# Fused attention and two MoE layers on one core: a second PSUM bank for the rows of w3·w_out, k of a head pair by one transfer, a scheduler that knows banks, and early operands for block 3

## Chip, cores and metric

One core of one Trainium2 chip. The metric is the device time of one launch in microseconds; three runs of the kernel before are given. TensorE's two clock levels are 1.2 and 2.4 GHz; the profile shows the granted share (1.00 is 2.4 GHz).

## The reference, cut

```python
attn_out = _attn_ref(q, k, v)            # (4, 8, 576, 64), block-causal, blocks of 64
x = attn_out.transpose(0, 2, 1, 3).reshape(2304, 512)
a, b = x @ w1, x @ w2                    # 512 -> 1024
h = a * b @ w3                           # 1024 -> 1024
y = h @ w_out                            # 1024 -> 512
r = np.maximum(y @ moe2_w_in, 0.0)       # 512 -> 2048
out = (r * r) @ moe2_w_out               # 2048 -> 512
```

The weights arrive as float64 and are taken apart on the chip into float32, and from there into a high and a low part.

## The kernel before

**Setup.** w3 and w_out are multiplied once: `setup_rows(i)` makes row block i (0 to 7) of w3·w_out, 128 x 512, by products of `w3_t[i]` with the eight pieces of w_out, accumulated in one PSUM bank. Rows 0 to 2 multiply in fp32 (8 products), rows 3 to 7 in three products of high and low parts each (24). Rows 0 to 5 (`PO_SPLIT = 6`) share the single buffer of tag `po`; of these rows 1 to 5 are made in two halves of 256 columns of that bank, each with its own eviction: ACT copies the high part into `w3o` (L1209), DVE the low part (L1214). Rows 6 and 7 take a bank from `bank3`, which goes round three banks: two of tag `tp`, one of tag `po`.

**Attention.** A head pair p (0 to 15) is loaded by `load_pair` (q, k, v; k as two transfers of 64 partitions, L627), its scores are made in groups of query tiles (`pair`), and pairs 0 to 3, those of batch b = 0, transpose their fp32 weights on TensorE: `transpose` makes for each pair, group and head a main and a last part, 48 tiles of tag `tp` with two buffers, each copied out by ACT (L974). Later pairs transpose by DMA. `attend` multiplies with v, into the bank `pv_bank`.

**First MoE.** `first_block(b)` makes a·b from the `w12` tiles (`ab`) and multiplies with the eight rows (`y`); y goes to DRAM. `w12_tile` converts w1 and w2; each has a small product on TensorE with column sums (`norm_scale`, L357, into `pv_bank`).

**Second MoE.** `second_block` goes over y in five blocks (`BLOCKS`: one of 256 tokens, c = 0, then four of 512). For c = 1 to 4 `h_winograd` makes seven products per pair j of weight tiles (`p17`, `p26`, `p45` with two halves each, `p3`) from operands that `y_load` splits out of y: `b11`, `b21`, `b22` and the differences `t1` to `t4`, each as a high part (ACT, L275) and a low part (DVE, L277). Each operand has one buffer. For c from 2 on the second product is `out_strassen` (`p1` to `p7` with a block number only). The products of `h_winograd` go round the three banks of `bank3`.

**What sets the order.** Nothing is issued as written. `Order.op` collects operations with an engine, an estimated cost, keys for what they read and write, and a priority; `Order.emit` then runs a list scheduler over all of them: on each engine it takes, among the operations whose inputs are ready at the earliest start, the one with the lowest priority key, and issues it. Each engine (and the queues of SP and POOL) then works in that order. `PE` work of low priority (rows, `ab`, `y`) fills where attention is not ready. `warm_up` puts idle matmuls of a zero tile where the scheduler sees TensorE idle in the first microseconds, into a buffer of tag `po`. An operation waits for a bank only through its keys: the two halves of a row have keys of their own, `(bank, half)`.

```python
        if not i:
            po_bank.append(buf("pm", "po", 1, [P, 512], F32, "po"))
        for half in range(2) if 0 < i < PO_SPLIT else (None,):
```

Of the kernel before, what the change touches and what calls it, by code (L numbers as in the profile page):

```python
# [7 lines left out]
F32 = mybir.dt.float32  # L8
F32R = mybir.dt.float32r
BF16 = mybir.dt.bfloat16  # L10
F16 = mybir.dt.float16
# [35 lines left out]

class Buf:
# [18 lines left out]
class Op:  # L67
    def __init__(self, eng, cost, fn, key, spare):
        self.eng, self.cost, self.fn, self.key, self.spare = eng, cost, fn, key, spare
        self.deps = set()  # L70
        self.left = 0
        self.users = []
        self.ready = 0.0
        self.end = None


class Order:
# [19 lines left out]
    def op(self, eng, cost, fn, r=(), w=(), key=0.0, spare=0.0):  # L97

        o = Op(eng, cost, fn, key, spare)
        o.same = self.same.get(eng, 0.0)  # L100
        for k in r:
            if k in self.writer:
                o.deps.add(self.writer[k])
            self.readers.setdefault(k, []).append(o)
        for k in w:
            if k in self.writer:
                o.deps.add(self.writer[k])
            o.deps.update(self.readers.pop(k, ()))
            self.writer[k] = o
        for k in list(r) + list(w):  # L110
            if isinstance(k[0], Buf):
                k[0].ops.append(o)
        o.deps.discard(o)
        self.ops.append(o)
        return o

    def emit(self):
# [11 lines left out]
        free, avail, dma = {}, {}, 0.0  # L129
        for n, o in enumerate(self.ops):  # L130
            o.n = n
            if not o.left:
                avail.setdefault(o.eng, []).append(o)
        count = 0
        while True:
            best = None
            for eng, todo in avail.items():
# [3 lines left out]
                start = max(t0, min(o.ready for o in todo))  # L141
                o = min((o for o in todo if o.ready <= start), key=lambda o: (o.key, o.n))
# [14 lines left out]
            else:  # L157
                free[eng] = start + o.cost
                o.end = free[eng] + self.TAIL.get(eng, 0.0)
            o.fn()  # L160
# [10 lines left out]
def fused_kernel(ctx: ExitStack, tc: tile.TileContext, qT, kT, vp, va, w12, w3t, wo, wb, out):  # L171
# [388 lines left out]

    raws = {}
# [20 lines left out]
    warm_out = buf("pm", "po", 1, [P, 512], F32, "warm_out")  # L582
# [33 lines left out]
    def load_pair(p):  # L616
# [7 lines left out]
        for a in range(2):  # L624
            rows = slice(64 * a, 64 * a + 64)
            od.op(
                GQ, c_dma(144), lambda rows=rows, n=2 * p + a: pool.dma_start(out=k()[rows], in_=kT[n][0:64]),  # L627
                [], [(k, a)], key,
            )
# [321 lines left out]
    def transpose(p, g, a, pf, weights, key):  # L951
# [7 lines left out]
        for part, (todo, n) in enumerate(((mains, P), (lasts, 64))):  # L959
            tp = buf("pm", "tp", 2, [P, 512], F32, f"tp_{name}_{part}")  # L960
# [154 lines left out]
    def bank3(name):  # L1115

        n_bank3[0] += 1
        tag, n = ("po", 1) if n_bank3[0] % 3 == 0 else ("tp", 2)
        return buf("pm", tag, n, [P, 512], F32, name)
# [53 lines left out]
    def setup_rows(i):  # L1173
# [4 lines left out]
        if not i:  # L1178
            po_bank.append(buf("pm", "po", 1, [P, 512], F32, "po"))
        for half in range(2) if 0 < i < PO_SPLIT else (None,):  # L1180
            cols = slice(0, 512) if half is None else slice(256 * half, 256 * half + 256)
            n = cols.stop - cols.start
            if i < PO_SPLIT:
                acc = Half(po_bank[0], cols, range(2) if half is None else (half,))
# [184 lines left out]
    def second_block():  # L1369
# [33 lines left out]
        ys_ = {}  # L1403
        raws_ = {}
        r_ = {}
        cp_ = {}

        def y_part(c, name):

            home = "wp" if name in ("b11", "b21") else "w2"  # L1410
            return [late(f"{name}{n}", [P, 2, TH], f"{name}{n}_{c}", F16, 1, home) for n in "hl"]

        def y_split(c, name, src, key):
            h, l = ys_[c, name] = y_part(c, name)
            split_half(h, l, src, 2 * TH, ([(h,)], [(l,)], [key]), K_EVICT)
# [106 lines left out]
        def y_load(c):  # L1522
# [17 lines left out]
            def sub(o, x, y, r, w):  # L1540
                od.op(
                    DVE, c_dve(2 * TH),
                    lambda: dve.tensor_tensor(out=o(), in0=x(), in1=y(), op=ALU.subtract), r, w, K_EVICT,
# [216 lines left out]
        def h_direct(c, j, key):  # L1760
            gt = g_half(c, j, f"g2_{c}_{j}")
            bt = beta_a if j < SOON else beta
            for k in range(2):
# [11 lines left out]
                ks = both(f, 0) + [(t,) for x in ("b11", "b21") for t in ys_[c, x]]  # L1775
# [66 lines left out]
        def h_winograd(c, j, key):  # L1842
# [16 lines left out]
            def product(acc, half, left, yname, spare=0.3):  # L1859
# [11 lines left out]
                od.op(PE, len(mms) * c_mm16(TH), go, ks + [(t,) for t in y], [(acc, half)], key, spare * strassen)  # L1871
# [30 lines left out]
            product(b17, 1, s_of(3), "t3")  # L1902
# [4 lines left out]
            product(b26, 1, s_of(2), "t2")  # L1907
            if strassen:
# [433 lines left out]
```

## Time and profile before

| | |
|---|---|
| three runs | 858.09, 859.74 and 859.10 us, median 859.1 us |
| the profiled execution | 859.63 us, of which the span from first to last instruction is 857.9 us |
| busy in the span | PE 834.0 us, PEld 676.9 us, DVE 704.3 us, ACT 605.3 us, POOL 111.4 us |
| granted TensorE clock, mean | 0.998 |

The profile is of one execution. Engines: PE TensorE's matmuls, PEld its weight loads (beside PE), DVE VectorE, ACT ScalarE, POOL GpSimd, SP the queue of SyncE. L12 is line 12 of the kernel before. An fp32 product is recorded as two matmuls. A time in brackets is idle time of the engine just before the row, with what ended it. PE's ends are modelled, so gaps under a few tenths of a microsecond do not show as idle.

### The profile page before, as it was taken

The numbers are of one execution on the slowest core, as the hardware profiler recorded it, in microseconds if no ns is written. First come the engines' busy times: TensorE is split into PE (matmuls) and PEld (weight loads), VectorE is DVE, ScalarE is ACT, GpSimd is POOL, SyncE is SP. The second block draws the span as 40 slices with busy tenths as digits, with TensorE's granted clock in tenths as the row PEclk, the third lists the DMA queues.
The fourth block names the chain that finished last, engine by engine and source line by source line (L and its number), as shares of the span: only waits on it lengthen the run. The fifth ranks groups of instructions, "written<-read, shape, count | busy, mean of one in ns | idle before, by whom it ended". The sixth has DMA issues, their size and how long they took to land. (4 is left out here: it accounts for less than half of the span.)

```text
span 857.9 us, 19317 instructions
## 1 busy us (share of the span) xinstructions
PE 834.0 (97%) x7504; PEld 676.9 (79%) x7504; DVE 704.3 (82%) x1643; ACT 605.3 (71%) x1393; POOL 111.4 (13%) x206
## 2 busy tenths in 40 slices
PE   8999999999999999999999999999999999999997
PEld 6567776778878888789979878666678888888886
DVE  5988989997787787864788899999979798797775
ACT  5988888976677676764999985756755654664562
POOL 5111211111211112001322101010020001001000
PEclk9999999999999999999999999999999999999999
DMA  8942465699998999772665512020030002001001
GB/s 312 339 150 93 135 176 161 143 182 191 215 178 159 196 154 202 134 148 77 210 193 191 176 50 74 26 100 2 1 109 16 1 2 74 2 1 51 1 2 50
DMA packets 104830, 100.23 MB, mean 117 GB/s; under 512 B 83041, under 2 KB 86881, under 8 KB 103329
## 3 DMA queue, kind: packets, MB, share of 16 engines
q0 software_dynamic: 18144, 71.18, 26.5%
q1 hardware_dynamic: 86592, 27.80, 19.1%
q8 instruction: 59, 0.97, 0.5%
q14 instruction: 35, 0.28, 0.1%
HBM read 62.78 MB, written 9.44 MB: 84 GB/s over the span
## 5 line engine op out<-in xcount | busy, mean ns | idle before, releaser
L1108 PEld LDWEIGHTS <-w 128*128 128x128 f16 x1536 | 146.8, 98 | 43.7 <-issue 5.9
L884 ACT ACTIVATE pf<-s,nm 128x192 f32<-128x192 f32 (+4 forms) x160 | 82.4, 524 | 44.0 <-DVE nm L867 39.5
L1108 PE MATMUL ab<-x0h,w 128*128 128x320 f16 x512 | 108.9, 299 | 0.5 <-DVE w L287 0.3
L1108 PE MATMUL y<-g,w3o 128*128 128x320 f32 (+1 forms) x768 | 108.3, 298 | 0.0
L1108 PEld LDWEIGHTS y<-g,w3o 128*128 128x128 f32 x768 | 103.1, 188 | 2.1 <-issue 1.2
L1108 PE MATMUL ab<-x1h,w 128*128 128x256 f16 x512 | 88.7, 273 | 0.0
L2034 PEld LDWEIGHTS <-gs 128*128 128x128 f16 x816 | 78.9, 98 | 11.4 <-DVE gs L277 2.2
L1866 PEld LDWEIGHTS <-wb 128*128 128x128 f16 x768 | 75.1, 98 | 15.2 <-issue 3.8
L1108 PE MATMUL ab<-x0l,w 128*128 128x320 f16 x256 | 76.5, 299 | 0.7 <-DVE x0l L1033 0.7
L1929 ACT ACTIVATE c<-c,beta 128x512 f32<-128x512 f32 x48 | 34.2, 713 | 58.4 <-DVE c L1898 58.4
L932 DVE SCALAR_TENSOR_TENSOR p<-pf,r,p 128x192 f16<-128x192 f32 (+2 forms) x120 | 63.0, 546 | 12.5 <-ACT p L925 11.2
L1108 PE MATMUL ab<-x1l,w 128*128 128x256 f16 x256 | 69.8, 272 | 0.0
L2161 PE MATMUL o<-wb,g 128*128 128x512 f16 x288 | 66.7, 379 | 0.6 <-DVE c L2171 0.6
L925 ACT ACTIVATE p<-pf,r 128x192 f16<-128x192 f32 (+2 forms) x120 | 62.0, 556 | 6.6 <-DMA pt<-p 3.7
L2034 PE MATMUL p<-ts,gs 128*128 128x256 f16 x480 | 61.8, 273 | 0.1
L1866 PEld LDWEIGHTS <-st 128*128 128x128 f16 x576 | 56.1, 98 | 6.7
L825 PE MATMUL s<-kraw,qraw 64*128 64x288 f32 (+4 forms) x384 | 56.5, 411 | 0.4 <-ACT pf L884 0.2
L2161 PEld LDWEIGHTS <-g 128*128 128x128 f16 x288 | 27.9, 98 | 30.3 <-issue 0.9
L825 PEld LDWEIGHTS s<-kraw,qraw 64*128 64x128 f32 x384 | 34.2, 186 | 17.1 <-issue 8.3
L2034 PE MATMUL p<-wb,gs 128*128 128x256 f16 x336 | 44.7, 273 | 0.2 <-DVE gs L277 0.2
L859 DVE TENSOR_REDUCE nm<-s 128x2 f32<-128x384 f32 (+1 forms) x64 | 42.3, 683 | 1.0
L338 DVE CUSTOM_DVE_ANT_0 cx<-raw,cx 128x1024 uint16<-128x1024 uint16 (+1 forms) x53 | 39.0, 737 | 4.5 <-ACT raw L329 2.3
(265 smaller groups left out, 1977.4 us busy)
## 6 DMA issues: line engine op xcount, KB each, us to landing
raw<-in_wb POOLq DMA_DIRECT2D x32, 512.0 KB, 5.5
raw<-in_w3t POOLq DMA_DIRECT2D x8, 1024.0 KB, 10.0
raw<-in_w POOLq DMA_DIRECT2D x16, 512.0 KB, 4.8
yraw<-ydram POOLq DMA_DIRECT2D x12, 512.0 KB, 4.5
vraw<-in_vp POOLq DMA_DIRECT2D x16, 320.0 KB, 5.3
qraw<-in_qT POOLq DMA_DIRECT2D x16, 288.0 KB, 4.7
kraw<-in_kT POOLq DMA_DIRECT2D x32, 144.0 KB, 5.9
vmix<-v SPq DMA_DIRECT2D x24, 160.0 KB, 5.0
```

The costliest lines, as they stand in the source:

```text
L338: dve.tensor_tensor(out=x(), in0=x(), in1=words()[1], op=ALU.add)
L825: pe.matmul(o[:, h] if t == 4 else o, q()[rows, q_start(t) : q_start(t) + 128], keys_()[rows, c], start=True, stop=True,)
L859: lambda k=k, t=t, nm=nm, banks=banks: dve.tensor_reduce(out=nm()[:, k], in_=banks[0]()[:, :, S_COL[t] : S_COL[t] + n_keys(t)], op=ALU.max ...
L884: act.activation(o, view(a, t), AF.Exp, bias=nm()[:, k, a : a + 1], scale=SCALE, accum_out=ssum()[:, k, a : a + 1],)
L925: lambda o=o, nk=nk, a=a, k=k, w=weights, p16=p16, r=r: act.activation(p16()[:, o : o + nk], w(a, k), AF.Copy, scale=r()[:, k, a : a + 1]),
L932: lambda o=o, nk=nk, a=a, k=k, w=weights, p16=p16, r=r: dve.scalar_tensor_tensor(out=p16()[:, o + nk : o + 2 * nk], in0=w(a, k), scalar=r( ...
L1108: pe.matmul(acc(), l, r, start=k == 0, stop=k == len(mms) - 1)
L1866: pe.matmul(acc()[:, TH * half : TH * half + TH], lhs(a, kc), y[yn]()[:, kc], start=n == 0, stop=n == len(mms) - 1,)
L1929: lambda src=src, k=k: act.activation(src(), src(), AF.Relu, scale=beta()[:, j, k : k + 1]),
L2034: pe.matmul(acc()[:, TH * u : TH * u + TH], t()[:, o : o + P], r(b), start=first and n == 0 and u == tiles[0], stop=last and n == 2 and u ...
L2161: pe.matmul(o(), g[gx]()[:, cols], wt(f)[:, a, 512:1024], start=(begin and n == 0), stop=(last and n == 2),)
```

## The change

1. Tag `po` has two buffers and tag `tp` one (`bank3` keeps its round over the three). Each of rows 0 to 5 takes a `po` buffer of its own and is made whole, 512 columns wide, with one eviction on ACT and one on DVE.
2. k of a pair is loaded by one transfer of 128 partitions; the bytes are the same.
3. `Order` notes which PSUM buffers an operation touches and starts none while another engine's operation on the same buffer runs.
4. Operands of blocks 3 and 4 are split at a priority inside the block before (`K_LOAD`) instead of the highest; block 3's `b11`, `b21` and `t3` get buffers of their own (`OTHER_HOMES`), so they need not wait for block 2's.
5. In `h_winograd` the product `t3` (second half of `p17`) is put behind both halves of `p26`.

```diff
+        o.banks = tuple(dict.fromkeys(k[0] for k in (*r, *w) if isinstance(k[0], Buf) and k[0].pool in PSUM_POOLS))
...
+        held = {}
+
+        def at(o):
+            t = o.ready
+            for b in o.banks:
+                for e, until in held.get(b, {}).items():
+                    if e != o.eng and until > t:
+                        t = until
+            return t
...
-                start = max(t0, min(o.ready for o in todo))
-                o = min((o for o in todo if o.ready <= start), key=lambda o: (o.key, o.n))
+                start = max(t0, min(at(o) for o in todo))
+                o = min((o for o in todo if at(o) <= start), key=lambda o: (o.key, o.n))
...
+            for b in o.banks:
+                held.setdefault(b, {})[eng] = o.end + self.WAIT
...
-    warm_out = buf("pm", "po", 1, [P, 512], F32, "warm_out")
+    warm_out = buf("pm", "po", 2, [P, 512], F32, "warm_out")
...
-        for a in range(2):
-            rows = slice(64 * a, 64 * a + 64)
-            od.op(
-                GQ, c_dma(144), lambda rows=rows, n=2 * p + a: pool.dma_start(out=k()[rows], in_=kT[n][0:64]),
-                [], [(k, a)], key,
-            )
+        both = slice(2 * p * P + P // 2, 2 * p * P + P // 2 + P)
+        od.op(GQ, c_dma(288), lambda: pool.dma_start(out=k(), in_=k_rows[both]), [], [(k, 0), (k, 1)], key)
...
-            tp = buf("pm", "tp", 2, [P, 512], F32, f"tp_{name}_{part}")
+            tp = buf("pm", "tp", 1, [P, 512], F32, f"tp_{name}_{part}")
...
-        tag, n = ("po", 1) if n_bank3[0] % 3 == 0 else ("tp", 2)
+        tag, n = ("tp", 1) if n_bank3[0] % 3 == 0 else ("po", 2)
...
-        if not i:
-            po_bank.append(buf("pm", "po", 1, [P, 512], F32, "po"))
-        for half in range(2) if 0 < i < PO_SPLIT else (None,):
+        if i < PO_SPLIT:
+            po_bank.append(buf("pm", "po", 2, [P, 512], F32, f"po_{i}"))
+        for half in (None,):
...
-                acc = Half(po_bank[0], cols, range(2) if half is None else (half,))
+                acc = Half(po_bank[i], cols, range(2) if half is None else (half,))
...
+        K_LOAD = [K_EVICT if c < 3 else K_B + 2 * (KP * (c - 1) + 5) + 0.55 for c in range(len(BLOCKS))]
...
+        OTHER_HOMES = {
+            "b11": ("wp", "ysq", 1, 1), "b21": ("wp", "ysc", 1, 1), "t3": ("mo1", "a", 2, 2),
+        }
...
-            split_half(h, l, src, 2 * TH, ([(h,)], [(l,)], [key]), K_EVICT)
+            split_half(h, l, src, 2 * TH, ([key_of(h)], [key_of(l)], [key]), K_LOAD[c])
...
             product(b17, 0, w_of(0, 0), "b11")
-            product(b17, 1, s_of(3), "t3")
...
             product(b26, 0, w_of(0, 1), "b21")
             product(b26, 1, s_of(2), "t2")
+            product(b17, 1, s_of(3), "t3")
```

The first place where the order moves is TensorE's queue at head pair 1 of the setup, from its first transposes on (`tp_1_0_0_0`: pair 1, group 0, head 0, main part; `po` a row of w3·w_out). Before:

```order
L968 MATMUL tp_1_0_0_0_535<-ident_92,pf_1_0_0_476 128x128 x3
L968 MATMUL tp_1_0_0_1_542<-ident_92,pf_1_0_0_476 64x128 x2
L968 MATMUL tp_1_0_1_0_552<-ident_92,pf_1_0_1_515 128x128 x3
L1108 MATMUL po_442<-wox_0_0_360,w3x_1_532 128x256
L1108 MATMUL po_442<-wox_0_1_382,w3x_1_532 128x256
L1108 MATMUL po_442<-wox_1_0_436,w3x_1_532 128x256
L1108 MATMUL po_442<-wox_1_1_440,w3x_1_532 128x256
L968 MATMUL tp_1_0_1_1_568<-ident_92,pf_1_0_1_515 64x128 x2
```

Now:

```order
L982 MATMUL tp_1_0_0_0_539<-ident_91,pf_1_0_0_421 128x128 x3
L1122 MATMUL po_1_548<-wox_0_0_339,w3x_1_504 128x512
L1122 MATMUL po_1_548<-wox_0_1_375,w3x_1_504 128x512
L982 MATMUL tp_1_0_0_1_562<-ident_91,pf_1_0_0_421 64x128 x2
L1122 MATMUL po_1_548<-wox_1_0_413,w3x_1_504 128x512
L1122 MATMUL po_1_548<-wox_1_1_415,w3x_1_504 128x512
L982 MATMUL tp_1_0_1_0_577<-ident_91,pf_1_0_1_464 128x128 x3
L1122 MATMUL po_1_548<-wox_2_0_451,w3x_1_504 128x512
L1122 MATMUL po_1_548<-wox_2_1_453,w3x_1_504 128x512
```

Two or more tiles of transposes that stood in a row are now parted by two products of a row, which are 512 columns wide. In the whole setup one of the 47 steps from a tile of transposes to the next has no other TensorE work between, where 21 had none.

The second place is VectorE's queue at the border from block 2 to block 3 (`c3_2_7`, `c3_3_0`: sums of block 2's last and block 3's first pair; `gs_1` operands of block 2's second product; `b11l` to `t4l` low parts of block 3's operands). Before:

```order
L277 TENSOR_TENSOR b11l_3_10076<-yraw_3_73_9433,b11h_3_10013 128x512
L277 TENSOR_TENSOR b21l_3_10085<-yraw_3_74_9421,b21h_3_10035 128x512
L1898 TENSOR_TENSOR c3_2_7_10024<-p3_2_7_10069,c3_2_7_10024 128x256
L277 TENSOR_TENSOR t1l_3_10096<-t1_3_9566,t1h_3_10059 128x512
L277 TENSOR_TENSOR t2l_3_10106<-t2_3_9595,t2h_3_10044 128x512
L277 TENSOR_TENSOR gs_1_9470<-c2_2_7_10057,gs_1_9470 128x512
L1543 TENSOR_TENSOR yraw_3_74_9421<-yraw_3_74_9421,t2_3_9595 128x2x256
L1940 TENSOR_TENSOR c3_2_7_10024<-c3_2_7_10024,c2_2_7_10057 128x256
L1898 TENSOR_TENSOR c3_3_0_10136<-p26_3_0_10117,x1_3_0_10125 128x256
L1940 TENSOR_TENSOR s23_2_7_10146<-c3_2_7_10024 128x512
L1898 TENSOR_TENSOR c3_3_0_10136<-p26_3_0_10117,x1_3_0_10125 128x256
```

Now:

```order
L294 TENSOR_TENSOR t1l_3_9975<-t1_3_9460,t1h_3_9955 128x512
L294 TENSOR_TENSOR t2l_3_9984<-t2_3_9490,t2h_3_9926 128x512
L1933 TENSOR_TENSOR c3_2_7_9928<-p3_2_7_9968,c3_2_7_9928 128x256
L294 TENSOR_TENSOR t4l_3_9995<-yraw_3_74_9313,t4h_3_9945 128x512
L294 TENSOR_TENSOR b22l_3_10005<-yraw_3_74_9313,b22h_3_9986 128x512
L294 TENSOR_TENSOR gs_1_9362<-c2_2_7_9958,gs_1_9362 128x512
L1975 TENSOR_TENSOR c3_2_7_9928<-c3_2_7_9928,c2_2_7_9958 128x256
L1975 TENSOR_TENSOR s23_2_7_10035<-c3_2_7_9928 128x512
L294 TENSOR_TENSOR gs_1_9362<-c3_2_7_9928,gs_1_9362 128x512
L1933 TENSOR_TENSOR c3_3_0_10052<-p26_3_0_10018,x1_3_0_10025 128x256 x2
```

`b11l`, `b21l` and the subtraction that makes `t4` (L1543) stand 36 to 55 rows earlier now, with `t3l`; `t4l` and `b22l` come before the sums of block 3. On TensorE `p45_3_0` is no longer parted: before, `p17_3_1` stood ahead of its half with `t4`; now the whole of `p17_3_0`, `p26_3_0` and `p45_3_0`, then `p1_2` and `p5_2`, and the first pair's last product, and `p17_3_1` comes only behind block 2's last output products. At the border from block 3 to block 4 the same moves stand. Between the attention of pair 10 and the end of block 0 of the second MoE, TensorE's order has not changed at all.

## Rows read from the trace of the kernel before

**Rows 1.** Busy by stretch: us, PE, PEld, DVE, ACT, POOL, clock, DMA share, GB/s.
```profile
25.00:50.00 25.00, 22.28 (x110) 14.20 (x112) 21.33 (x47) 22.40 (x47) 2.58 (x4) 0.93 0.74 272
50.00:75.00 25.00, 24.03 (x188) 19.13 (x185) 21.67 (x43) 22.55 (x48) 4.20 (x7) 1.00 0.30 101
75.00:100.00 25.00, 23.54 (x202) 18.83 (x202) 21.30 (x59) 20.03 (x56) 4.58 (x9) 1.00 0.34 110
...
125.00:150.00 25.00, 23.10 (x184) 17.36 (x183) 24.24 (x66) 20.79 (x47) 3.62 (x7) 1.00 0.63 174
150.00:175.00 25.00, 23.79 (x263) 18.76 (x261) 23.50 (x63) 22.53 (x61) 3.80 (x7) 1.00 0.70 151
...
250.00:425.00 175.00, 175.00 (x1925) 147.51 (x1920) 125.99 (x321) 122.18 (x326) 26.34 (x51) 1.00 0.78 158
...
675.00:700.00 25.00, 23.75 (x219) 21.09 (x217) 23.04 (x48) 15.52 (x30) 0.00 (x0) 1.00 0.01 1
750.00:775.00 25.00, 23.71 (x217) 20.82 (x216) 23.04 (x47) 15.56 (x30) 0.00 (x0) 1.00 0.00 1
```

**Rows 2.** Waits of TensorE, whole span: us in total, times, longest.
```profile
PE p L1866 <- DVE c L1898: 2.9, 3, 1.3
PE tp L968 <- DVE pf L910: 2.4, 3, 1.6
PE po L1108 <- DVE w3o L1214: 2.4, 5, 0.6
PE tp L968 <- ACT pt L974: 2.1, 3, 1.4
PE pv_bank L357 <- DVE wsum L406: 1.7, 2, 1.3
PE pv_bank L357 <- ACT junk L413: 1.6, 2, 1.1
...
PE po L1108 <- ACT w3o L1209: 0.5, 1, 0.5
```

**Rows 3.** The tile tp: durations min/median/max in ns, first and last start.
```profile
L974 ACT ACTIVATE pt<-tp x48: 255/450/610, 13.0 to 109.8; 128x384 f32<-128x384 f32 x16, 64x256 f32<-64x256 f32 x8, 64x192 f32<-64x192 f32 x8, 128x512 f32<-128x512 f32 x8
```

**Rows 4.** Timeline of TensorE: fp32 row, a row in halves, a whole row.
```profile
32.06 3.79 PE L1108 MATMUL po<-wox,w3x 128*128 128x512 f32 x8
...
69.69 1.68 PE L1108 MATMUL po<-wo,w 128*128 128x256 f32 x12
...
113.97 7.28 PE L1108 MATMUL po<-wo,w 128*128 128x512 f32 x30
```

**Rows 5.** Groups by form, 24 to 125 us: busy us, mean ns.
```profile
L1108 PE MATMUL po<-wo,w 128*128 128x256 f32 x144 | 21.4, 292 | 1.0 <-DVE w3o L1214 1.0
...
L1108 PE MATMUL po<-wo,w 128*128 128x512 f32 x48 | 12.0, 402 | 0.0
...
L478 ACT ACTIVATE raw<-raw 128x1024 f32<-128x1024 f32 x5 | 5.9, 1186 | 0.0
```

**Rows 6.** Stretches around the half clock, columns as in rows 1.
```profile
35.60:39.20 3.60, 1.94 (x11) 1.30 (x11) 3.60 (x8) 3.60 (x6) 0.02 (x1) 1.00 1.01 280
39.20:42.60 3.40, 3.40 (x10) 2.55 (x9) 2.46 (x4) 2.02 (x5) 0.53 (x1) 0.50 0.35 147
```

**Rows 7.** Timeline, 0 to 30 us: the first loads of k.
```profile
1.96 1.05 POOL L627 DMA_DIRECT2D kraw<-in_kT  x2
...
6.22 1.91 PEld L825 LDWEIGHTS s<-kraw,qraw 64*128 64x128 f32 x14 [0.25 <-DMA kraw<-in_kT]
```

**Rows 8.** Timeline of VectorE and TensorE at the two block borders.
```profile
687.29 0.68 DVE L277 TENSOR_TENSOR b11l<-yraw,b11h 128x512 f16<-128x512 f32 x1
687.88 0.68 DVE L277 TENSOR_TENSOR b21l<-yraw,b21h 128x512 f16<-128x512 f32 x1
...
690.63 0.68 DVE L1543 TENSOR_TENSOR yraw<-yraw,t 128x512 f32<-128x512 f32 x1
...
692.50 0.41 DVE L1898 TENSOR_TENSOR c<-p,x 128x256 f32<-128x256 f32 x1
...
692.96 0.27 PE L1866 MATMUL p<-b11h,wb 128*128 128x256 f16 x1 [1.25 <-DVE c L1898]
...
768.09 0.27 PE L1866 MATMUL p<-b11h,wb 128*128 128x256 f16 x1 [1.29 <-DVE c L1898]
```

More of the change, by code (lines that the diff above doesn't have):

```diff
@@ L45, in n_keys @@
     return 128 * t + 64
+PSUM_POOLS = ("ps", "pm", "mb")
 class Buf:
@@ L70, in __init__ @@
         self.deps = set()
+        self.banks = ()
         self.left = 0
@@ L1406, in second_block, with __init__, __call__, key_of @@
         cp_ = {}
-        def y_part(c, name):
+        OTHER_HOMES = {
+            "b11": ("wp", "ysq", 1, 1), "b21": ("wp", "ysc", 1, 1), "t3": ("mo1", "a", 2, 2),
+        }
+        class Piece:
+            def __init__(self, b, n):
+                self.b, self.n, self.key = b, n, (b, n)
+            def __call__(self):
+                return self.b()[:, self.n]
+        def key_of(t):
+            return t.key if isinstance(t, Piece) else (t,)
+        def y_part(c, name):
+            if c == FIRST_S + 1 and name in OTHER_HOMES:
+                *home, pieces = OTHER_HOMES[name]
+                if pieces == 2:
+                    return [buf(*home, [P, 2, TH], F16, f"{name}{n}_{c}") for n in "hl"]
+                t = buf(*home, [P, 2, 2, TH], F16, f"{name}_{c}")
+                return [Piece(t, n) for n in range(2)]
             home = "wp" if name in ("b11", "b21") else "w2"
@@ L1542, in sub @@
                     DVE, c_dve(2 * TH),
-                    lambda: dve.tensor_tensor(out=o(), in0=x(), in1=y(), op=ALU.subtract), r, w, K_EVICT,
+                    lambda: dve.tensor_tensor(out=o(), in0=x(), in1=y(), op=ALU.subtract), r, w, K_LOAD[c],
                 )
@@ L1773, in go @@
                         )
-                ks = both(f, 0) + [(t,) for x in ("b11", "b21") for t in ys_[c, x]]
+                ks = both(f, 0) + [key_of(t) for x in ("b11", "b21") for t in ys_[c, x]]
                 od.op(PE, len(mms) * c_mm16(TH), go, ks, [(acc,)], key)
@@ L1869, in go @@
                         )
-                od.op(PE, len(mms) * c_mm16(TH), go, ks + [(t,) for t in y], [(acc, half)], key, spare * strassen)
+                od.op(PE, len(mms) * c_mm16(TH), go, ks + [key_of(t) for t in y], [(acc, half)], key, spare * strassen)
             if strassen:
```

1 line of the change is left out of this document (added).

## Prediction

> **What bounds the kernel now.** I read the busy time by stretch first, then TensorE's waits, then the timelines of the places they name. Busy by stretch [rows 1] shows TensorE filled without a gap from 250 to 425 us, while VectorE and ScalarE have 49 us and more to spare in those 175. In the setup, 25 to 175 us, no engine is full and all three are near it: TensorE 22 to 25 of 25, VectorE 21 to 24, ScalarE 20 to 22.5. TensorE is thus the bound wherever it has work, and what a change can win is TensorE's idle time (857.9 - 834.0 = 23.9 us in all) and TensorE work that can go. Since its order is word for word the same from the attention of pair 10 up to the end of block 0 of the second MoE, whatever is won or lost in the setup should pass through that stretch as one shift of all engines.
>
> The waits [rows 2] say who ends the idle time. Two entries are this change's own: the bank of the rows, po, 2.4 + 0.5 = 2.9 us in six waits, and the products of the second MoE that wait for VectorE, 2.9 us in three. The transposes wait 2.1 us for their copies with two buffers, 2.4 us for weights that VectorE has still to scale; the small products of the w12 conversions wait 1.7 + 1.6 = 3.3 us.
>
> **The change part by part.** The sum is against the profiled execution, 859.63 us (span 857.9 and 1.7 around it), which lies 0.5 above the median of the runs.
>
> *Two banks for the rows.* A row's products no longer wait until the row before (or its other half) is copied out. The six waits [rows 2] go: -2.9 us; nothing else is late there, as the second bank has been free for a whole row's work. The ends: 0, if TensorE only comes earlier to its next wait, and -2.9.
>
> *Whole rows instead of halves.* Twelve products of 256 columns take 1.68 us, 0.14 each; thirty of 512 take 7.28, 0.243 each [rows 4]. So 512 columns cost 0.28 in halves and 0.243 whole. Rows 3 to 5 are 144 halves [rows 5], 72 whole: 72 x (0.28 - 0.243) = 2.7 us. The 1.68 holds the tail of its last product, which the next work covers; busy time by form bounds it from above: 21.4 against 72 x 12.0/48 = 18.0 [rows 5], 3.4 us. I take 1.7, half of that, as part of these halves filled time in which the attention wasn't ready anyway; ends 0 and -3.4. Rows 1 and 2 are fp32, where the columns set the time: nothing. Five evictions fewer on ScalarE and on VectorE are beside TensorE's work and count as nothing; if that cover went they would be a gain.
>
> *One buffer for transposes.* There are 48 tiles, each copied out in 0.26 to 0.61 us, 0.45 in the middle [rows 3]. Now each must be copied before the next starts. Most steps have row products between: two fp32 ones, four records of 3.79/8 = 0.47 us, 1.9 in all, or six others, 6 x 0.243 = 1.5 [rows 4]. That is more than copy and hand-over; but ScalarE, in order, may have conversions of 1.19 us [rows 5] queued ahead of the copy. The one wait of this kind seen is 1.4 [rows 2]. I take +1.5 us: the 2.1 of now stays, and three more waits of half a microsecond come. Ends: -0.6 (the spacing of the new order ends some of the 2.1) and +9.6 (the slower rival below).
>
> *The w12 conversions.* TensorE comes to their small products earlier by what it has won, and VectorE, which has 24.24 of 25 us busy at 125 to 150 and 23.50 in the next stretch [rows 1], can't follow at once. The 3.3 us of waits [rows 2] grow: I take +1.0; ends 0 and +4.6 (all of the two row terms is waited for again).
>
> *k by one transfer.* Two issues on POOL take 1.05 us [rows 7], one some half of it; POOL is busy under 5 us of 25 in the setup's stretches [rows 1], so 15 of the 16 are hidden. The first pair's are not: its first products wait 0.25 us for the second half of k [rows 7]. -0.2; ends -0.5 (the whole issue) and +0.5 (the first half's products now wait for the whole).
>
> *Early operands.* At each border TensorE stops, 1.25 and 1.29 us, until VectorE has made the second sum of block 3's first pair at 692.50, for the bank that `p17_3_1` wants [rows 8]; ahead of it VectorE made four low parts and one subtraction of 0.68 us. Walked through in the new order with these durations: `t4l` ends near 689.5, `p45_3_0` needs it at 691.6; `gs_1` from the first sum ends near 692.6, `p1_2` needs it at 692.9; the second sum of the first pair still ends near 693, but nothing asks for its bank before `p3_3_0`, 1.3 us later. So both stops go but for some 0.2 each: -2.1 us. What is late next is `gs_1` from the last sums, for `p6_2`, by up to 0.2, within that. The work moved forward, three ScalarE and four VectorE instructions per block, lies where VectorE has 2 us of 25 to spare [rows 1]. Ends: 0 (the stop moves to `p6_2`) and -2.5.
>
> *The product t3 later, and the scheduler that knows banks.* The order of blocks 1 to 4 changes by one product; the same products run. The third wait of the 2.9 us, 0.4, may go or another of its size come: 0, ends -1 and +1.
>
> *The clock.* From 39.2 to 42.6 us the granted clock is 0.50, that is 1.2 GHz, after a stretch in which TensorE was busy 1.94 of 3.60 us [rows 6]. TensorE worked all of those 3.4 us, at half speed: 1.7 us lost. The same sparse stretch may be filled now or fall elsewhere: 0, ends -1.7 and +1.7.
>
> Sum: -2.9 - 1.7 + 1.5 + 1.0 - 0.2 - 2.1 = -4.4 us, so 855.2 against the profiled execution and **854.7** against the median.
>
> For the second bank a page of the Trainium skill speaks against the gain: "TensorE: Matmul & The Clock Gate", section "HAM oscillation — how this bites in real kernels", reports of one kernel that double-buffering in PSUM gave no further gain. By that the sum would be -1.5. The trace doesn't agree so far, as it shows six waits that a copy out of the one bank ended [rows 2]; no run here shows it yet.
>
> **The rivals.**
>
> *The single transposing bank costs more than all that is won (slower).* For it: ScalarE is at 22.4 and 22.55 of 25 us where the transposes run [rows 1], and the new order queues conversions between the copies of one tile's main and last part. With two of 1.19 us [rows 5] and a copy of 0.45 [rows 3] ahead of it, less the 1.9 us of row products [rows 4], a transpose waits 2.4 + 0.45 - 1.9, or some 0.9 us, 0.8 where the second has begun. Without the transposes the sum is -5.9, so it decides from eight such waits of the 47 on. With twelve, +9.6: 859.1 - 5.9 + 9.6 = 862.8 us. Against it: only one step has no other TensorE work between, where 21 had none before.
>
> *The setup's gain is waited for again.* If VectorE sets the pace from 125 to 175 us [rows 1], TensorE stands before the w12 conversions as long as it came early, and the borders alone remain: 859.1 - 2.1 = 857.0 us. For it: 24.24 of 25. Against it: VectorE and ScalarE lose 3 to 5 of 25 us in the three stretches before, some of that waiting for TensorE.
>
> *The second bank wins nothing.* Six waits end in the same place for another reason (the next row's weights are not converted): 859.1 - 1.5 = 857.6 us. For it: w3's conversions run beside the rows. Against it: each wait is ended by a copy of po [rows 2].
>
> *The operands don't come early enough (the change doesn't do what it says).* Only `b11`, `b21` and `t3` have other homes; `t1`, `t2`, `t4` and `b22` still wait for block 2's last products, and if `t4l` is late by a microsecond the stop stays: 859.1 - 2.3 = 856.8 us. Against it: 2 us of room for `t4l` in the walk above.
>
> **How the numbers follow.** About 0.2% (1.7 us) is what a measurement of this kernel can tell from no change. Chances: forecast 0.57, the slower rival 0.12, setup waited for again 0.17, second bank nothing 0.06, operands late 0.08. The forecast's own ends, with the terms not all at one side, are 851 to 857.3. The range reaches below by the clock's 1.7 less something, 850.5, and above to 859.8, which takes in all rivals but the slower one. Faster by over 0.2% (under 857.4): nearly all of the forecast, some two thirds of the second and third rivals together, most of the last: 0.74. Within 0.2%: 0.15. Slower: 0.11, the slower rival but for its mild end.
>
> **What would show it.** Right: no wait of po for w3o; rows of 512 columns, 0.24 us a record; waits of transposes for their copies between 2 and 5 us; w12 waits of 3 to 5 us; no TensorE gap above 0.3 us at the two borders, near 688 and 762 us; the first `ab` of batch 1 some 2 to 3 us earlier and everything up to the second MoE shifted alike. Wrong, if the transposes wait for their copies over 6 us in total, if the w12 waits take 6 us, if a gap of a microsecond stands at a border under another tile's name, or if the shift at 250 us is not there at 500.

## The result and the profile after

The changed kernel takes 848.33 us (median of four runs, 847.93 to 848.49) beside 858.96 of the kernel before in the same comparison: a ratio of 0.9876, 95% interval 0.9859 to 0.9893. It is 10.6 us faster. I forecast 4.4 us (854.7, range 850.5 to 859.8), so the sign was right and the size was outside the range. The profiled execution has 848.49 us, a span of 846.7, and a mean granted clock of 0.999.

TensorE's waits in the kernel after (us in total, times, longest) answer to [rows 2]:

```profile
PE tp L982 <- ACT pt L988: 3.0, 6, 1.1
PE pv_bank L374 <- DVE wsum L423: 2.4, 3, 1.4
PE tp L982 <- DVE pf L924: 1.6, 1, 1.6
PE y L1122 <- DVE a L1284: 1.1, 1, 1.1
...
PE pv_bank L374 <- ACT junk L430: 0.5, 1, 0.5
...
PE o L2196 <- DVE c L2206: 0.4, 1, 0.4
```

The list has no product of a row that waits for a copy any more, and the three waits of `p` for VectorE's `c` are gone. Transposes wait 3.0 us for their copies instead of 2.1, and the products of the w12 conversions 2.4 + 0.5 = 2.9 instead of 3.3. Busy time by stretch, columns as in [rows 1]:

```profile
25.00:50.00 25.00, 23.75 (x123) 12.47 (x124) 23.18 (x48) 25.00 (x49) 3.23 (x6) 1.00 0.78 282
...
125.00:150.00 25.00, 23.67 (x190) 17.84 (x188) 24.45 (x68) 23.67 (x59) 3.23 (x6) 1.00 0.86 180
150.00:175.00 25.00, 25.00 (x272) 19.48 (x269) 22.17 (x57) 19.90 (x52) 3.24 (x6) 1.00 0.83 170
...
675.00:700.00 25.00, 24.93 (x229) 22.05 (x227) 23.56 (x48) 14.01 (x26) 1.83 (x3) 1.00 0.09 29
750.00:775.00 25.00, 25.00 (x231) 22.31 (x229) 21.26 (x44) 12.42 (x23) 1.59 (x3) 1.00 0.06 23
```

The two stretches with the block borders are full now (24.93 and 25.00 of 25), where TensorE had 23.75 and 23.71. To see where the 11.2 us of span went I cut both traces at the same two events: the start of the last record of scores (the attention's last products of q and k) and the first product of block 1 of the second MoE. Before, then after:

```profile
0.00:373.42 373.42, 358.26 (x3422) 282.70 (x3422) 307.27 (x787) 288.17 (x753) 66.95 (x127) 1.00 0.79 182
373.42:544.08 170.66, 170.06 (x1507) 143.74 (x1503) 133.23 (x317) 137.12 (x313) 30.95 (x57) 1.00 0.44 134
544.08:857.90 313.82, 305.65 (x2581) 250.47 (x2579) 263.83 (x542) 180.03 (x330) 13.49 (x22) 1.00 0.09 30
```

```profile
0.00:366.07 366.07, 353.72 (x3319) 270.85 (x3319) 305.89 (x782) 287.35 (x748) 57.41 (x111) 1.00 0.77 186
366.07:536.18 170.11, 170.06 (x1507) 143.76 (x1503) 133.46 (x317) 137.04 (x313) 31.32 (x57) 1.00 0.44 134
536.18:846.70 310.52, 305.16 (x2581) 251.29 (x2579) 262.87 (x542) 181.13 (x330) 13.46 (x22) 1.00 0.09 30
```

7.35 us were won up to the last scores, 0.55 in the rest of the first MoE, 3.30 from there on. My sum had 2.3, 0 and 2.1. So it is the setup that was mis-sized, and that is what the experiments are about.

### The profile page after: what moved, and what is told of

The parts are those of the page before. It is cut to its first block, busy times and chain, and to the rows that moved or that the text cites. A ratio compares the mean times of both kernels' runs of the same rounds, so it can differ in the third digit from the quotient of the medians.

```text
span 846.7 us, 19113 instructions
## 1 busy us (share of the span) xinstructions
PE 828.9 (98%) x7401; PEld 665.9 (79%) x7401; DVE 702.2 (83%) x1638; ACT 605.5 (72%) x1388; POOL 102.2 (12%) x190
## 4 chain that ended last, share of the span: by engine, by line
PE 57%; DVE 8%; ACT 7%; issue 2%; DMA 1%; POOL 0%; DVEq 0%; POOLq 0%; ACTq 0%
PE ab L1122 13%; PE p L1901 11%; PE y L1122 9%; PE p L2069 9%; PE o L2196 6%; PE pv_bank L1031 3%; PE s L839 3%; PE h L1805 2%; DVE c L1933 2%; ACT c L1964 2%; DMA raw<-in_wb 1%; ACT c L1967 1%; DVE gs L294 1%; DVE c L1975 1%; DVE s L1975 1%
## 5 line engine op out<-in xcount | busy, mean ns | idle before, releaser
L292 ACT ACTIVATE gs<-c 128x512 f16<-128x512 f32 (+1 forms) x56 | 29.9, 535 | 18.2 <-DVE c L1975 18.0
```

Source lines behind the costliest of these rows:

```text
L292: od.op(ACT, c_act(n), lambda: act.activation(hi(), src(), AF.Copy), ks, kh, key)
```

## The experiments

All kernels are set against runs of the kernel before in the same comparison, with a 95% interval of the ratio. "Scores" is the start of the last record of scores in the kernel's profile, "half" the time in us at a granted clock of 0.50 (1.2 GHz) before that point; the profiles of `a_k2` and `a_v330` have 3.4 us of it behind that point, at 377.9 us.

| kernel | median us | ratio | scores | half |
|---|---|---|---|---|
| before | 858.5 to 859.4 | 1 | 373.4 | 3.4 |
| b_rows: before + part 1 | 857.82 | 0.9997 (0.9988 to 1.0005) | 368.0 | 3.4 |
| b_k1: before + part 2 | 857.34 | 0.9985 (0.9969 to 1.0001) | 371.3 | 0 |
| b_rowsk: before + parts 1, 2 | 852.35 | 0.9925 (0.9913 to 0.9937) | 366.9 | 3.4 |
| b_rows_k1same | 858.12 | 0.9987 (0.9966 to 1.0008) | 368.0 | 3.4 |
| after | 848.33 | 0.9876 (0.9859 to 0.9893) | 366.1 | 0 |
| after2: the same again | 848.56 | 0.9880 (0.9865 to 0.9894) | 367.6 | 3.4 |
| a_k2: without part 2 | 853.77 | 0.9957 (0.9940 to 0.9973) | 367.0 | 0 |
| a_k2same | 849.92 | 0.9886 (0.9857 to 0.9916) | 367.7 | 0 |
| a_v310: planner's figure for v -3% | 850.75 | 0.9905 (0.9877 to 0.9932) | 367.0 | 6.8 |
| a_v330: planner's figure for v +3% | 855.44 | 0.9958 (0.9943 to 0.9973) | 366.6 | 0 |
| a_half2: two banks, halves | 848.69 | 0.9874 (0.9847 to 0.9902) | 366.2 | 3.4 |
| a_half2_warm | 848.12 | 0.9887 (0.9873 to 0.9902) | 364.4 | 0 |
| a_whole1: one bank, whole rows | 851.93 | 0.9915 (0.9886 to 0.9944) | 369.1 | 3.4 |
| a_whole1_v310 | 854.53 | 0.9949 (0.9932 to 0.9965) | 369.3 | 3.4 |
| a_half1: without part 1 | 861.18 | 1.0034 (1.0014 to 1.0055) | 387.5 | 23.9 |
| a_half1_nobank: without parts 1, 3 | 855.00 | 0.9948 (0.9934 to 0.9963) | 373.3 | 3.4 |
| a_late: without part 4 | 852.51 | 0.9920 (0.9895 to 0.9944) | 367.4 | 3.4 |
| a_t3: without part 5 | 850.10 | 0.9893 (0.9869 to 0.9916) | 366.3 | 0 |
| a_nobank: without part 3 | 848.80 | 0.9880 (0.9857 to 0.9903) | 366.0 | 0 |

### Parts 1 and 2, alone and together

`b_rows` puts part 1 of the diff above into the kernel before, and nothing else; `b_k1` part 2, `b_rowsk` both.

```diff
...
-        for half in range(2) if 0 < i < PO_SPLIT else (None,):
...
+            po_bank.append(buf("pm", "po", 2, [P, 512], F32, f"po_{i}"))
+        for half in (None,):
...
```

> The kernel before with part 1 alone: two po banks, one tp bank, whole rows. Theory A (the 7.35 us that the change won up to 250 us come from the rows' part: 2.9 us of waits for po, some 3 us less TensorE work in rows, 1.7 us of half clock that goes with the denser stretch): 6 to 8 us faster than before, no half-clock stretch. Rival B (they come from k's single transfer): 2 us faster at most, the half clock still there. Rival C (they belong to no part: each part sends the scheduler down another order): anything, and the parts alone do not add up to the whole.

> The kernel before with parts 1 and 2: rows and k by one transfer. All theories: about 7.4 us faster than before, since the rest of the change is said to act on the second MoE alone. A: no more than 0.5 us away from part 1 alone. B: 5 us faster than part 1 alone. C: several us away from part 1 alone in either direction.

> The kernel before with part 2 alone: k of a pair by one transfer. A: within 0.5 us of before. B: 4 to 7 us faster. C: a shift of a microsecond or more of either sign, with another order of the setup.

Part 1 alone is worth 0.7 us by medians and part 2 alone 1.1, and neither interval tells that from nothing; both together are worth 6.1. Theory A fell, and so did B; C's mark, that the parts don't add up, is what was seen. The traces cut as above, part 1 alone and then both parts:

```profile
0.00:367.97 367.97, 354.14 (x3311) 270.58 (x3311) 303.62 (x777) 283.98 (x743) 67.39 (x127) 1.00 0.78 185
367.97:541.97 174.00, 172.20 (x1517) 145.13 (x1515) 139.17 (x331) 141.28 (x320) 30.90 (x57) 1.00 0.42 131
```

```profile
0.00:366.88 366.88, 355.38 (x3318) 272.13 (x3319) 306.14 (x782) 287.48 (x748) 57.34 (x111) 1.00 0.77 185
366.88:536.80 169.92, 169.87 (x1506) 143.68 (x1503) 133.43 (x317) 137.36 (x313) 31.09 (x57) 1.00 0.44 135
```

Up to the last scores part 1 alone is already 5.45 us ahead of before (373.42 - 367.97). It loses 3.3 of that in the rest of the first MoE, 174.00 against 170.66: 12 records of `ab` more are still to do there (some 1.6 us, at three records in 0.41 us of that timeline), and TensorE stands idle 1.8 us (174.00 - 172.20) instead of 0.6; the remaining half microsecond wasn't traced. The timeline of part 1 alone shows where (lines are of that kernel; brackets: idle time before):

```profile
373.37 3.35 PE L1125 MATMUL y<-g,w3o 128*128 128x320 f32 x21
...
375.62 1.44 ACT L942 ACTIVATE p<-pf,r 128x576 f16<-128x576 f32 x2
...
377.16 0.55 DVE L1287 SCALAR_TENSOR_TENSOR a<-ab,ab_back,a 128x320 f32<-128x320 f32 x1
...
377.74 0.47 ACT L261 ACTIVATE g<-a 128x320 fp32r<-128x320 f32 x1 [0.68 <-DVE a L1287]
...
378.27 0.42 PE L1125 MATMUL y<-g,w3o 128*128 128x320 f32 x1 [1.54 <-ACT g L261]
```

`y` stops after 21 records, because the last `ab` was made just before it and the copy of its result stands behind the attention's work on ScalarE and VectorE. With both parts attention products stand between the last `ab` and this `y`, and its first 35 records stand in one group:

```profile
370.86 5.41 PE L1122 MATMUL y<-g,w3o 128*128 128x320 f32 x35
```

What part 2 changed at this place is the order; whether the transfer has a price of its own is the next question.

### The transfer or the order

`a_k2same` issues two transfers that the planner counts as one: TensorE, VectorE, ScalarE and SyncE keep the changed kernel's order word for word. `b_rows_k1same` is the reverse, in the order of part 1 alone. `a_k2` undoes part 2 altogether.

```diff
...
+        def k_two(k=k, p=p):
+            for a in range(2):
+                pool.dma_start(out=k()[64 * a : 64 * a + 64], in_=kT[2 * p + a][0:64])
...
+        od.op(GQ, c_dma(288), k_two, [], [(k, 0), (k, 1)], key)
```

> The changed kernel with k of a pair loaded by two transfers again, but planned as one: TensorE, VectorE, ScalarE and SyncE work in exactly the changed kernel's order, and only POOL issues one transfer more per pair. New theory D (k's single transfer is worth nothing as a transfer; what it gives beside the rows' part, 5.5 us, is another order of the setup that the planner's figures lead to): within 0.8 us of the changed kernel. Rival B (the transfer itself): 4 to 6 us slower.

> The kernel before with part 1, k by one transfer, but planned as two: the order of part 1 alone on four engines. D: within 0.8 us of part 1 alone (857.8). B: 4 to 6 us faster than that.

> The changed kernel with part 2 undone, planned as it was before: k of a pair by two transfers that the planner counts as two. The chip moves the same bytes as with a_k2same (849.9), where TensorE kept the changed kernel's order; here TensorE's order is within 16 rows of a_v330's (855.4). D (the order alone): 854 to 857 us, so 5 us or more above a_k2same. If two transfers cost the same however they are planned: 849 to 851.

> The changed kernel itself once more, as the bar for the others of this call: 847.9 to 849 us. If a_k2same's 849.9 was the transfer's own price and not scatter, this stays 1 us or more below it.

The same bytes in the same two transfers take 849.9 us in the changed kernel's order and 853.8 in the order that two transfers, planned as two, lead to: 3.9 us by the order alone, and the intervals lie apart. The transfer itself is worth nothing that can be measured in the order of part 1 alone (858.1 against 857.8) and some 1.4 to 1.6 in the changed kernel's (849.9 against 848.3 and 848.6), where the intervals overlap, but the profile of `a_k2same` is 1.6 us later at the last scores with no half clock in either. That is outside theory D's 0.8 us, and by the mark set for `after2` (1 us or more) the transfer does have a price in this order; the order has the larger one. `a_k2` came out 0.2 us under its forecast.

### Other orders of the same work

```diff
-        od.op(GQ, c_dma(320), lambda: pool.dma_start(out=v(), in_=vp[p]), [], [(v,)], key)
+        od.op(GQ, c_dma(330), lambda: pool.dma_start(out=v(), in_=vp[p]), [], [(v,)], key)
```

> The changed kernel with one figure of the planner changed: it takes the transfers of v for 3% shorter (310 instead of 320). Nothing else is changed, and the chip's work is the same but for its order in the setup and the first MoE. D, taken to its end (the order alone is a matter of several us, whatever leads to it): 2 to 8 us slower or, less likely, as much faster. If orders are worth little: within 1.5 us.

> The changed kernel with the planner's figure for transfers of v 3% longer (330 instead of 320). This gives TensorE almost the order (16 rows apart) that two transfers of k, planned as two, would give. D (the order alone): 3 to 6 us slower than the changed kernel, as part 1 alone was 5.5 us slower than parts 1 and 2. If the changed kernel's setup is good for what its banks are: within 1.5 us.

One figure of the planner, 3% down or up, costs 2.4 and 7 us (3 to 6 were expected for the second). The same instructions run, in another order. At 330 most of the loss comes behind the last scores. They are 0.6 us later than in the changed kernel (366.63 and 366.07), but from there to the first product of block 1 it takes 176.13 us where the changed kernel takes 170.11. Of these 6.0 us, 12 records of `ab` that are still to do take some 1.6; the wait of `y` for `g` stands again, near 377, and the half clock follows it:

```profile
PE y L1122 <- ACT g L261: 1.5, 1, 1.5
```

`a_k2` has the same there: 175.67 us, a wait of 1.5, the half clock behind it. In the setup weight loads for transposes wait longer at 330, 12.3 us in 22 times for ScalarE's copies, where the changed kernel has 9.0 in 15 (below). Of the three orders drawn by this figure the changed kernel's is the fastest.

### Width

`a_half2` keeps both banks and makes rows 1 to 5 in halves.

```diff
-        for half in (None,):
+        for half in range(2) if 0 < i < PO_SPLIT else (None,):
```

> The changed kernel with both po banks, but rows 1 to 5 in halves of 256 columns again. Theory A's part on widths (whole rows save TensorE work): 2.5 to 3.5 us slower. If the width saves nothing, because the halves filled time in which the attention wasn't ready: within 1 us. D says that the reordering, which ends before the first MoE's middle, may add 1 to 3 us of either sign to this.

848.69 against 848.33 and 848.56: with two banks the width is worth nothing that can be measured (with one bank it is, see the next part). Two rows of the timeline before and two of after show why, when starts are taken instead of the modelled durations of [rows 4]:

```profile
65.83 1.67 PE L1108 MATMUL po<-wo,w 128*128 128x256 f32 x12
67.43 2.33 PE L1071 MATMUL pv_bank<-pt,vraw 128*64 128x128 f32 x36
```

```profile
83.38 1.67 PE L1122 MATMUL po<-wo,w 128*128 128x512 f32 x6
84.89 0.27 PE L982 MATMUL tp<-ident,pf 128*64 128x128 f32 x1
```

Twelve halves take 1.60 us from start to next start, 0.133 each, or 0.267 for 512 columns; six whole ones 1.51, 0.252. Over 72 pairs that would be 1.1 us, and next to nothing where the twelve take 1.52 us (69.69 to 71.21 in that timeline).

### The second bank

`a_whole1` and `a_whole1_v310` have one `po` bank and two `tp` banks with whole rows; `a_half1` undoes part 1, `a_half1_nobank` also part 3.

```diff
-            po_bank.append(buf("pm", "po", 2, [P, 512], F32, f"po_{i}"))
+            po_bank.append(buf("pm", "po", 1, [P, 512], F32, f"po_{i}"))
...
-            tp = buf("pm", "tp", 1, [P, 512], F32, f"tp_{name}_{part}")
+            tp = buf("pm", "tp", 2, [P, 512], F32, f"tp_{name}_{part}")
```

> The changed kernel with whole rows in one po bank, and two tp banks. If the second po bank matters by itself: each of five rows waits for both evictions of the row before, 0.6 + 0.7 us and hand-over, unless other work stands between: 2 to 6 us slower, with waits of po for w3o. If other work hides them: within 1 us. Theory D: the other order decides, a few us of either sign, and the po waits explain less than half of it.

> The changed kernel with one po bank and two tp banks, whole rows, and the planner's figure for v at 310. Another draw of an order with one bank for the rows. If the second bank is worth something in any order: 851 to 856 us, above each draw with two banks (848.3, 848.7, 850.75). If only the order counts: anywhere from 847 to 856, and as often below 850.75 as above.

> The changed kernel with part 1 undone: one po bank, two tp banks, rows 1 to 5 in halves; the rest kept. A: 5.5 to 7.5 us slower than the changed kernel, with the po waits back. B: within 2 us of the changed kernel. C: slower by another amount than part 1 alone gains.

> The changed kernel with parts 1 and 3 undone, that is the kernel before with k by one transfer, early operands and t3's new place. Its setup is in the order of part 2 alone (857.3), so 857.3 - 3.3 = 854.0 us. It tells what made the kernel without part 1 so slow (861.2): if knowing banks with one bank for halves did it, this is 6 to 8 us faster than that; if the missing second bank did, it stays at 859 to 861.

The orders with two banks give 848.3, 848.7, 850.75 and 855.4 us (with k by two transfers 849.9 and 853.8), those with one 851.9, 854.5, 855.0 (without part 3) and 861.2: the two groups overlap. At the last scores all kernels with two banks are at 364.4 to 368.0, those with one at 369.1 to 373.4 (and `a_half1` at 387.5); up to 18 records of `ab`, 2.5 us, lie on the other side of this mark in some. Counted in at 0.137 us each, they put `b_rows` (369.6) and `a_v310` (369.5) behind `a_whole1` (369.1). So the second bank goes with a gain there in every order drawn against rows in halves, and not in every one against whole rows.

Four kernels keep parts 2 to 5 and differ in the bank and the width alone: one bank with halves 861.2, one bank with whole rows 851.9, two banks with halves 848.7, two with whole rows 848.3. The second bank is worth 12.5 us with halves and 3.6 with whole rows, the width 9.3 us with one bank and 0.4 with two. The two edits overlap: each takes away most of what the other could, and what either is worth can't be said without the other. (The orders differ with each edit, and the 861.2 holds the planner's part and more half clock as well, below.)

The nearest pair is `a_half1_nobank` and `a_half2`, both with halves and with 3.4 us of half clock, apart in the banks and in part 3 (which leaves TensorE's order in the setup alone where there are two banks): 373.26 against 366.20, 7.1 us. The waits for copies that the first one's trace lists are 3.5 us in seven (2.1 + 1.4). More may hide in the records of the rows, which are the same in number and form in both. First one bank, then two (mean ns; after the bar the idle time before them):

```profile
L1122 PE MATMUL po<-wo,w 128*128 128x256 f32 x144 | 22.1, 294 | 1.9 <-DVE w3o L1228 1.0 <-ACT w3o L1223 0.9
L1122 PE MATMUL po<-wox,w3x 128*128 128x256 f32 x64 | 16.4, 392 | 1.6 <-DVE w3o L1228 1.2 <-ACT w3o L1223 0.5
```

```profile
L1122 PE MATMUL po<-wo,w 128*128 128x256 f32 x144 | 20.4, 289 | 0.0
L1122 PE MATMUL po<-wox,w3x 128*128 128x256 f32 x64 | 15.5, 383 | 0.0
```

38.5 us against 35.9: 2.6 us look like waiting that is counted as busy, since an end is modelled. The Trainium skill says the same of the ends (page "Perfetto Trace Analysis", section "Tensor Engine Instruction (MATMUL, LD_WEIGHTS)": estimated, not observed). But the whole rows in the same two kernels go the other way, 19.5 us (11.8 + 7.7) against 20.7 (12.9 + 7.8), so busy time doesn't settle it. Starts do. From 20 us to the last scores I add up what each step from one TensorE start to the next lasts beyond the median step behind a record of that form, where that is over 0.1 us. Ahead of products of rows this is 9.3 us in 44 steps with one bank and 1.3 in 11 with two; ahead of transposes 3.2 and 5.7. So 8.0 us are won at the rows and 2.5 paid at the transposes; that is 5.5 of the 7.1, and the rest lies in steps ahead of other products. With whole rows it is 4.7 us at the rows with one bank (`a_whole1`) and 1.5 with two. And from the kernel before to the changed one it goes from 8.3 to 1.5 at the rows and from 4.5 to 5.5 at the transposes. One stop in the kernel before:

```profile
44.13 1.03 PE L1108 MATMUL po<-wox,w3x 128*128 128x256 f32 x4
...
45.20 0.38 ACT L1209 ACTIVATE w3o<-po 128x256 fp32r<-128x256 f32 x1 [0.81 <-PE po L1108]
...
45.63 1.13 PE L1108 MATMUL po<-wox,w3x 128*128 128x256 f32 x4 [0.47 <-ACT w3o L1209]
46.87 0.42 DVE L1214 TENSOR_TENSOR w3o<-po,w3o 128x256 fp32r<-128x256 f32 x1 [1.59 <-PE po L1108]
...
47.35 0.48 PE L1108 MATMUL po<-wox,w3x 128*128 128x256 f32 x1 [0.59 <-DVE w3o L1214]
```

Both copies hold TensorE's rows up, each in turn, though the halves have keys of their own. The Trainium skill asks for that (page "PSUM — Partial Sum Buffer", section "PSUM bank collisions raise a hardware error": PSUM is to be guarded by bank and quarter of the partitions, or simply by bank, not by address). The trace shows that it is kept here, not what would happen otherwise: in the kernel before, of the 22 copies of rows 0 to 5 and their halves out of the one bank, no product of a row starts during the first 20, and during the last two only those of row 6, which has another bank; with two banks in `a_half2` products of rows start during 14 of all 26 copies. The price is on the transposes' side. Weight loads for them wait for ScalarE's copies as follows, before and after (us, times, longest):

```profile
PEld tp L968 <- ACT pt L974: 3.3, 4, 1.7
```

```profile
PEld tp L982 <- ACT pt L988: 9.0, 15, 1.2
```

Part 3 belongs to the second bank. With one bank and halves, a planner that knows banks costs 6.2 us (861.2 against 855.0); the profile of `a_half1` is of its longest run, 867.3 us, and has 23.9 us of half clock. With two banks it wins 0.4 in the second MoE (below), and nothing that the medians show (848.80).

### The second MoE

```diff
-        K_LOAD = [K_EVICT if c < 3 else K_B + 2 * (KP * (c - 1) + 5) + 0.55 for c in range(len(BLOCKS))]
+        K_LOAD = [K_EVICT for c in range(len(BLOCKS))]
...
-            if c == FIRST_S + 1 and name in OTHER_HOMES:
+            if c < 0 and name in OTHER_HOMES:
```

`a_late` has this, `a_t3` has t3 back in its old place, `a_nobank` takes `o.ready` for `at(o)` in the scheduler's choice.

> The changed kernel with part 4 undone: operands of blocks 3 and 4 split at the highest priority and in their own single buffers only. The setup's order is the changed kernel's. Theory E (early operands take away the two border gaps): 2.0 to 2.6 us slower, with gaps of 1.2 to 1.3 us back where blocks 3 and 4 begin; from the first product of block 1 to the last of block 4 some 308.4 us where the changed kernel takes 306.05. Rival (the gaps went by t3's new place or by the scheduler that knows banks): under 0.8 us.

> The changed kernel with part 5 undone: t3 in its old place, ahead of both products of p26. If t3's place matters beside the early operands: gaps at the borders come back in part, 0.5 to 2 us slower. If it is worth nothing, as I counted it: within 0.4 us from the first product of block 1 to the last of block 4.

> The changed kernel with part 3 undone: a scheduler without banks. TensorE's order is the same up to the middle of the second MoE. Theory: the 0.32 us gap where block 2 begins returns, and little else, 0.3 to 0.8 us slower. Rival (knowing banks makes the borders, or the setup): 1.5 us slower or more.

From the first product of block 1 to the last of block 4 the three take 309.3, 307.0 and 306.5 us, where the changed kernel takes 306.05 and the one before 309.26. Theory E holds: without early operands the whole 3.2 us is lost, and the gap stands at the border again, ended by the same sum (1.29 us here, 0.88 at the next border):

```profile
685.98 0.76 DVE L1933 TENSOR_TENSOR c<-p,x 128x256 f32<-128x256 f32 x2
...
686.79 0.27 PE L1901 MATMUL p<-b11h,wb 128*128 128x256 f16 x1 [1.29 <-DVE c L1933]
```

t3's place counts for 0.95 and the planner's banks for 0.4; together that is more than the 3.2 there are, so they overlap, and why was not taken apart. `a_late`'s median is 4.2 us above the changed kernel's, more than the 2.6 expected; its profile has 3.4 us of half clock in the setup. t3's place, which I had counted at nothing, is in the range of the other theory.

### The clock

`a_half2_warm` puts 18 more idle matmuls where TensorE waits for the first weights to transpose.

```diff
...
+            warm_cost.append(n)
             warm_cost[0] = 0.062
+            if len(warm_cost) == 3:
+                n += 18
```

> The changed kernel with both banks and rows 1 to 5 in halves (848.7), and 18 more idle matmuls of the zero tile in the 1.6 us in which TensorE waits for the first weights to transpose, near 11 us; all other instructions in the same order. In its profile 3.4 us of half clock began 1.5 us after that wait, and two profiles of the changed kernel, one with and one without such a stretch, differ by 1.6 us at the last scores. If the sparse stretch brings it on: no half clock before 370 us, 847 to 848 us. If not: 848.7, the half clock still there.

The profile has no half clock before the end and the earliest last scores of all, 364.37; the median, 848.12, is not to be told from 848.3 or 848.7. Its first transposes also come 1.14 us earlier than `a_half2`'s (11.40 and 12.54), so of the 1.83 us at the last scores at most 0.7 go with the clock. It is the fastest by its median, but I don't call it faster than the changed kernel.

## Why the prediction was wrong

**The setup as a sum of terms (-2.3 us, measured -7.35) is the step that failed**, in two of its terms and in adding them up.

*Two banks, "the ends: 0 ... and -2.9".* The listed waits were no bound. From start to start, what held up the products of rows went from 8.3 us to 1.5, 6.8 us where the forecast had 2.9 for the waits and 1.7 for the width. The mechanism, a copy that holds up the rows, was right; the size was too small, and the wait and the width were added up though they act on the same stops: with one bank whole rows were worth 9.3 us (861.2 to 851.9), with two nothing measurable. Against the forecast's doubt, the Trainium skill's page "TensorE: Matmul & The Clock Gate" (section "HAM oscillation — how this bites in real kernels") reports of one kernel that double-buffering in PSUM gave no further gain. That is what part 1 alone gave, 0.7 us, and not what the nearest pair shows, 6.3 us in the medians (855.0 to 848.7).

*k by one transfer, "-0.2; ends -0.5 ... and +0.5".* I priced the transfer and not what the planner makes of it. Undone, part 2 costs 5.4 us: 3.9 by the order, up to 1.6 by the transfer. No term of mine stood for the order, and the finished order beside that of before doesn't tell which part moved what.

The other steps:

- *Whole rows, -1.7*: as less work for TensorE nothing measurable, as the starts of records show; I took the modelled end of a group for its length. The five evictions fewer, at nothing, stand: `a_half2` has them back.
- *One transposing buffer, +1.5*: near enough. PE's waits grew by 0.9, the steps ahead of transposes by 1.0, the weight loads' waits by 5.7. The slower rival didn't come, though at another planner's figure those waits went to 12.3 us.
- *w12, +1.0*: wrong in sign, 3.3 us became 2.9. The rival in which the setup's gain is waited for again is, in part, what befell part 1 alone, by another wait, of `y` for `g` (1.2 us more idle time of the 3.3 lost). The "3 to 5 of 25 us" that VectorE and ScalarE lose in the three stretches before are 2.45 to 4.97 in [rows 1]; nothing rests on it.
- *Early operands, -2.1*: right in kind and 1.1 to 1.2 us short: 3.2 to 3.3 us with t3's place and the banks, which I had at 0.
- *The clock, 0*: before had 3.4 us of half clock in the setup [rows 6], and this profile of after has none there. By the changed kernel's two profiles (last section) that is some 1.0 us of the profiled 11.2, an estimate; what it is in the medians is not shown.
- Of the signs named beforehand, the waits of transposes, the borders and the rigid shift came as said, and the w12 waits were just under their mark (2.9 where 3 to 5 was said); the first `ab` came 10.8 us earlier (113.09 against 123.87) instead of 2 to 3, as the rows are now made between the transposes: the last product of a row starts at 112.75 and the last transpose at 112.98, where before the rows went on to 123.63 behind the last transpose at 108.41.

Open is how much of the 7.1 us is the bank at an unchanged order, and why the two edits overlap to the degree they do. That wasn't tried, because the buffers' number goes into the planner and changes the order with it.

## What to carry to other kernels

Where a list scheduler makes the order, price an edit by the order that it leads to and not by its own work: build each part alone and together, keep the order while changing the work, and shift a planner's figure by a few per cent to see how wide orders scatter (here 7 us, two thirds of the whole gain). Waits that a trace lists for TensorE were under half of what a blocked bank cost here (3.5 us listed, 8.0 from start to start); compare the starts of the same records in a kernel without the block. And try two edits that act on the same wait in all four combinations before adding up their prices.

## What was not expected of the hardware

Stretches of half clock of 3.4 us come and go between runs of one kernel. The changed kernel's two profiles are in the same order; one has its first transposes 0.6 us later and 3.4 us of half clock behind them, and is 1.57 us later at the last scores (367.64 and 366.07). Columns as in [rows 1], from the wait for the first transposes on; first with the half clock, then without:

```profile
10.20:12.36 2.16, 0.53 (x11) 0.39 (x8) 1.70 (x7) 2.16 (x11) 1.16 (x3) 1.00 1.03 411
...
13.60:17.00 3.40, 3.40 (x23) 2.41 (x21) 2.94 (x10) 2.46 (x4) 1.65 (x4) 0.51 1.00 358
```

```profile
10.20:11.74 1.54, 0.00 (x0) 0.03 (x1) 1.08 (x6) 1.54 (x9) 1.07 (x3) 1.00 1.03 408
...
13.60:17.00 3.40, 2.94 (x41) 2.48 (x39) 3.40 (x9) 2.76 (x6) 1.13 (x3) 1.00 1.02 387
```

Ahead of it TensorE was idle 1.6 us in both. Of the 1.57 us, 0.62 are there before the clock falls, so the half clock goes with about 1.0. The Trainium skill (page "TensorE: Matmul & The Clock Gate", section "What's actually happening") says that how many matmuls run at the lower clock at a kernel's start differs from run to run of one kernel; the two profiles, with the half clock at 13.65 us in one of them, agree. `b_k1` and `a_half1_nobank`, also in one order up to there, differ by 1.96 us for 3.4 us of half clock, 0.43 of it by the first transposes (11.76 and 12.19). So what comes and goes between two profiles of one kernel can be worth a third of an expected gain (1.57 of 4.4), and two profiles are compared only after the clock and the start of the first transposes are looked up.
